# Linear attention into routed experts, one core: transfers, stores and weights sent at other points of the steps, and the placing of a group, one-hots and the late table rearranged

## The chip, the cores and the metric

The kernel runs on one core of a Trainium2 chip. The metric is the time of one execution on the device, in microseconds; lower is better. Engines are named as in the profile: PE (TensorE), PEld (its weight loads), DVE (VectorE), ACT (ScalarE), POOL (GpSimd), SP (SyncE, which here only sends DMAs).

## The reference, cut to what matters

```python
# q, k, v, alpha: (4, 8, 768, 48)
for t in range(S):
    state = alpha[:, :, t, :, None] * state + k_t (outer) v_t
    y[:, :, t] = q_t @ state
x = y as rows: (3072, 384)
skip = x @ w_skip                       # rows with skip <= 0 pass unchanged
e_idx = argmax(x @ w_gate); gate = softmax value at e_idx     # 8 experts
out = x + gate * (relu(x @ w1[e]) @ w2[e])                    # w1: 384x1024, w2: 1024x384
```

All of it is fp32; products run as fp32 (two passes of PE) or as two-term splits (`h` and `l` tiles).

## The kernel before, in words

**Attention.** The 4 x 768 positions are 24 tiles of 128 (`NT`), two batches interleaved, six chunks each; a tile holds all eight heads as four pairs. One loop of `static_path` (L1042) takes a tile i a step and writes the order of every engine by hand. A step holds on PE: `inter` (old state times queries, not in the first chunk), `intra(i, 0)` (first half of scores times values), `scores(i + 1)`, `intra(i, 1)`, `rows(i - 1)` (back to rows, with gate logits), `outer(i)` and `turn_k(i + 1)` (the state's update, not in the last chunk). DVE has `decay` for tile i + 3 in two parts: part 0 scans the decays forward (`pfx`) and POOL scales the queries by it (L281), part 1 scans backward (`sfx`) and POOL scales the keys (L290). Without these keys `scores` of that tile can't start. `causal` (DVE, L321) masks the scores of tile i + 1 into `st`, for which `intra(i + 1, 0)` waits. ACT copies PSUM to SBUF.

**Transfers.** A tile has rows (`qka`: decays, keys, queries; 0.595 MB in two DMAs, `load` parts 0 and 1) and values (`vt`, 0.197 MB, part 3); a finished tile of x is stored (0.197 MB). All go out by SP, in the order of the code. `plan(i)` counts PE's products (an fp32 matmul counts two) and at product 221 + 127n + 4 calls `issue(i, behind)`, whose DMAs wait for that product: rows and values of tile i + 5 (`AHEAD`), then the store of tile i - 2; from step 19 on, where no tiles are left, three pieces of weights (`weight_loads`, 0.262 MB each) instead. `weight_loads` is a generator whose first call sets `self.wait` to None (L656). The prologue sends tiles 0 to 4 without such waits.

**Routing.** The rows fall into groups of tiles, (0, 6), (6, 12), (12, 18), and then late ones, (18, 21), 21, 22, 23. `route` finds the expert (mask `m`) and the gate, six and eight small DVE instructions, handed out by `tick`. `rank` (PE) and `place` (DVE, three instructions) give each row its slot; `one_hot` turns a tile's slots into a 128 x 256 matrix, `marks` spreads ids and gates, and `table` multiplies the two on PE into the table of slots (two small matmuls a tile). A one-hot takes DVE or POOL. `early_rows` gathers expert 0's rows of the first 18 tiles from the table by an indirect DMA of POOL; the late tiles' rows come by `mine` (DVE) and `late_rows` (PE) straight into the first product's input, for which `late_split` makes two-term splits (ACT, POOL). `clear_late` stores zeros over tile 22's rows.

**Experts.** Then each expert is `up`, `down` with weights loaded ahead, split on ACT, DVE and POOL.

Of the kernel before, what the change touches and what calls it, by code (L numbers as in the profile page):

```python
# [10 lines left out]
F32 = mybir.dt.float32  # L11
# [6 lines left out]
ALU = mybir.AluOpType  # L18
# [12 lines left out]
NT = B * C  # L31
NQ = 6
AHEAD = 5
# [33 lines left out]
LATE = 18  # L67
SOLO = 12
EG = 8
WARM = 36  # L70
BLOCK0, BLOCK, PAST, STEP = 221, 127, 4, 112
ORDER = (0, 2, 4, 1, 3, 5)
FIRST = 512
PAUSE = "pause"
# [2 lines left out]
class Kernel:  # L77
# [166 lines left out]
    def load(self, i, part=None, behind=None, eng=None):  # L244
        nc = self.nc
        if i >= NT:
            return
        if part is None:
            for n in range(4):
                self.load(i, n)  # L250
            return
        if part == 0:
            t = self.qkab[i % NQ]
            vt = self.vp.tile([P, DM], F32, name="vt")
            self.work[i] = dict(dec=t[:, 0:DEC], v=vt, qh=t[:, QO:QW].rearrange("p (a t) -> p a t", t=P),
                                kh=t[:, KO:QO].rearrange("p (a t) -> p a t", t=P), begun=set())
        if part == 3:
            ins = (eng or nc.sync).dma_start(out=self.work[i]["v"], in_=self.v[i])
        elif part >= len(WHOLE.get(i, USED)):
            return  # L260
        elif i not in WHOLE:
            rows = USED[part]
            ins = nc.sync.dma_start(out=self.qkab[i % NQ][rows], in_=self.qka[i, rows])
        else:
            s = slice(*WHOLE[i][part])
            ins = (eng or nc.sync).dma_start(out=self.qkab[i % NQ][:, s], in_=self.qka[i, :, s])
        if behind:
            self.follow(ins.ins, behind)
# [265 lines left out]
    def place(self, g):  # L534

        nc = self.nc
        g0, g1 = g
        n = g1 - g0
        pr = self.ranks(g)
        if g0 < LATE:  # L540
            sl = self.sm.tile([P, GT, E], F32, name="sl")[:, :n, :]
        else:
            sl = self.lates[:, g0 - LATE:g1 - LATE, :]
        s2 = self.pslot[:, g0 - SOLO:g1 - SOLO, :] if g0 in (SOLO, NT - 2, NT - 1) else \
            self.late.tile([P, n, 1], F32, name=f"s{g0}")
        for i in range(g0, g1):
            self.work[i]["slot"] = s2[:, i - g0, :]
            self.work[i]["slot0"] = sl[:, i - g0, 0:1]
        yield nc.vector.scalar_tensor_tensor(out=sl, in0=pr, scalar=-BIG, in1=self.m[:, g0:g1, :], op0=ALU.add,
                                             op1=ALU.mult)  # L550
        yield nc.vector.tensor_reduce(out=s2, in_=sl, op=ALU.add, axis=AX.X)
        if g0 < LATE:
            yield nc.vector.memset(pr, 0.0)
# [14 lines left out]
    def marks(self, g):  # L568
        g0, g1 = g
        wide = [P, g1 - g0, E, VW]  # L570
        eng = self.nc.vector if g0 >= SOLO else self.nc.gpsimd
        eng.tensor_tensor(self.mv[:, g0:g1], self.m[:, g0:g1, :].unsqueeze(3).to_broadcast(wide),
                          self.values(g).unsqueeze(2).to_broadcast(wide), ALU.mult)

# [44 lines left out]
    def late_split(self, i, direct=False):  # L619
        nc, w = self.nc, self.work[i]  # L620
        hi, lo = w["parts"] = [self.late.tile([P, DM], F32R, name=f"late{n}{i}") for n in "hl"]
        nc.scalar.copy(out=hi, in_=w["x"])
        if direct:
            pairs = lambda a: a.rearrange("p (a w) -> p a w", a=NP)
            nc.vector.tensor_tensor(pairs(lo), pairs(self.pg[:, 0:NP * RW])[:, :, 0:2 * D], pairs(hi).bitcast(F32),
                                    ALU.subtract)
        else:
            nc.gpsimd.tensor_tensor(lo, w["x"], hi.bitcast(F32), ALU.subtract)

    def late_rows(self, i, ks):  # L630
        w = self.work[i]
# [22 lines left out]
    def weight_loads(self):  # L654

        self.raw, self.wait = {}, None  # L656
        for e in range(E):
            for name, src in (("w1", self.w1), ("w2", self.w2)):
                raw = self.raw[e, name] = self.wraw.tile([P, KT * F], F32, name="raw")
                soon = (e, name) < (1, "w2")  # L660
                step = FIRST if soon else KT * F // 4
                for q in ORDER if name == "w1" and soon else range(KT * F // step):
                    s = slice(q * step, (q + 1) * step)
# [6 lines left out]
    def weight_splits(self):  # L670
# [5 lines left out]
        for e in range(E):  # L676
            for name in ("w1", "w2"):
# [5 lines left out]
                if e == 0 and name == "w1":  # L683
                    yield
                    continue
                for q in ORDER if name == "w1" else range(6):
                    s = slice(q * step, (q + 1) * step)
# [275 lines left out]
    def static_path(self, ctx):  # L963
        tc, nc = self.tc, self.nc
# [3 lines left out]
        self.stay = ctx.enter_context(tc.tile_pool(name="stay", bufs=1))  # L968
        self.banks(ctx)
        loads, splits = self.weight_loads(), self.weight_splits()  # L970
        small = []
        groups = [(0, 6), (6, 12), (12, 18), (18, 21), (21, 22), (22, 23), (23, 24)]

        def advance(it, n=1):
            for _ in range(n):
                next(it, None)

        def tick(n):
            while n and small:
                r = next(small[0], self)  # L980
                if r is self:
                    small.pop(0)
                elif r is PAUSE and n < 50:
                    break
                else:
                    n -= 1

        def bring(i, parts, behind):
            for n in parts:
                self.load(i + AHEAD, n, behind)  # L990

        def issue(i, behind):
            if i + AHEAD < NT:
                bring(i, (0, 1, 3), behind)
            else:
                self.wait = behind
                advance(loads, 3)
            if i < 20:
                self.store(i - 2)

        def plan(i):
            begin = self.products
# [4 lines left out]
        with ExitStack() as st:  # L1007
# [17 lines left out]
                self.load(3, n)  # L1025
            self.load(1, 3)
            self.row_weights()
            self.load(2, 3)
            self.load(4)
            self.load(3, 3)  # L1030
            self.fill(WARM)
            self.scores(0)
            self.cross(0)
# [8 lines left out]
            for i in range(NT):  # L1042
# [2 lines left out]
                    plan(i)  # L1045
                self.inter(i)
                self.intra(i, 0)
                self.fence(i)
                if i:
                    self.keep(i - 1)  # L1050
# [12 lines left out]
                self.scores(i + 1)  # L1063
                self.cross(i + 1)
                if i == 22:
                    self.table((11, 15, 16, 17))
                    self.table_add()
                    self.early_rows(self.numbers(self.tab[:, :, 0:1, :], "ids0", 1))
                self.causal(i + 1)
                if i == 22:  # L1070
                    for _ in self.route(groups[3], True):
                        pass
                tick(2)
                self.decay(i + 3, 0)
                self.intra(i, 1)
                if i == 1:
                    bring(i, (0, 1), self.work[i]["before"])
                self.turn_y(i)
# [3 lines left out]
                    self.logits(i - 1)  # L1082
                if i >= 19:
                    self.store(i - 1)
                if i == 19:
                    self.clear_late(self.work[i - 1]["rowed"])
                self.outer(i)
                if i == 1:
                    bring(i, (3,), self.work[i]["added"])
                if 11 <= i < 22:  # L1090
                    self.table((10, 12, 13, 14) if i == 21 else (i - 11,))
                for g in groups[:3]:
                    if i == g[1] + (2 if g[0] == SOLO else 3):
                        self.rank(g)
                self.carry(i)
                for g in groups[:3]:
                    if i == g[1] + (2 if g[0] == SOLO else 3):
                        for _ in self.place(g):
                            pass
# [4 lines left out]
                tick(1)  # L1104
                if i == 20:
                    tick(99)
                    self.marks(groups[2])
                    for t in range(3):
                        self.one_hot(SOLO + t, nc.vector)
                self.decay(i + 3, 1)  # L1110
                for g in groups[:3]:
                    if i == g[1]:
                        small.append(self.route(g))
                if i in (9, 15):
                    tick(99)
                    self.marks(groups[{9: 0, 15: 1}[i]])
                if 9 <= i < 21:
                    self.one_hot(i - 9, nc.gpsimd)
                if i == 21:
                    for t in range(3):  # L1120
                        self.one_hot(SOLO + 3 + t, nc.vector)
                if i == 11:
                    self.table_add(first=True)
                if i == 22:
                    self.route_one(21)
                tick({18: 6}.get(i, 2))
                if i > LATE:
                    self.late_split(i - 1)
                if i == 19:
                    advance(splits)  # L1130
                if 19 <= i < 23:
                    self.first_split(ORDER[i - 19:i - 18])
                if i == 22:
                    self.first_split((2, 4), nc.gpsimd)
                if i == 21:
                    self.first_split((0,), nc.vector)
                if i == 1:
                    self.rank_constants()
                if i == 2:
# [17 lines left out]
            self.wait = self.ranked  # L1157
            advance(loads, 3)
            self.store(a)
            advance(loads, 2)  # L1160
            self.late_rows(18, range(KT))
            put(g21)
            self.mine(21)
            self.route_one(22)
            self.late_split(22)
            self.first_split((3, 5))
            self.rows(b)
            self.logits(b)
# [9 lines left out]
            self.mine(a)  # L1178
            self.row_copy(b)
            self.store(b)  # L1180
            advance(loads, 2)
            self.late_split(b, True)
            self.early_turn()
            self.late_rank(g23)
# [100 lines left out]
```

## Time and profile before

| | |
|---|---|
| three runs | 267.28, 264.58, 267.57 us, median 267.28 |
| profiled execution | 265.31 us, span 263.6 us |
| busy: PE, PEld, DVE, ACT, POOL | 94%, 88%, 75%, 63%, 67% of the span |
| granted clock of TensorE | 0.993 on average |
| DMA | 59.97 MB, 228 GB/s on average |
| chain that ended last | PE 84%, issue 4%, DVE 4%, POOL 3%, DMA 2% |

The chain follows the work back from the last instruction to what released it; "issue" is time in which the engine waited for nothing that the profile shows. The stages differ: the steps run to about 109 us, the hand-over to 119.7, the experts from there on.

### The profile page before, as it was taken

What the parts mean: (1) busy time and instruction counts of PE and PEld (TensorE: products, weight loads), DVE (VectorE), ACT (ScalarE), POOL (GpSimd) and SP (SyncE); (2) the same over time, 40 slices, a digit from 0 to 9 for tenths busy, and PEclk for the clock granted to TensorE, in tenths of its full rate; (3) what the DMA queues carried; (4) which work ended last, traced back from release to release, by engine and by line L of the source; (5) the groups of instructions that cost most, each with busy time, mean ns of one, the idle gap of its engine ahead of it and who ended that gap; (6) DMA issues with size and microseconds to landing.
All of it is one profiled execution on the core that took longest, in us unless ns stands there. A gap on an engine that the chain in (4) does not pass through costs nothing.

```text
span 263.6 us, 9702 instructions
## 1 busy us (share of the span) xinstructions
PE 247.4 (94%) x3988; PEld 231.6 (88%) x3988; DVE 197.1 (75%) x389; ACT 166.4 (63%) x356; POOL 177.3 (67%) x197
## 2 busy tenths in 40 slices
PE   8679999988999988999999999999999999999990
PEld 6569898976899877789999999999999999999990
DVE  6978889999799889888957728559568496674800
ACT  8657576656567577543646499695995974644600
POOL 6757775779598885999774764848568366546411
PEclk9999999999999999999999999999999999999997
DMA  7987887779788887773499949778698777421000
GB/s 235 325 249 218 278 230 245 216 239 294 223 230 229 266 253 237 218 236 99 133 358 334 323 152 396 267 261 325 196 396 306 228 247 288 152 117 43 3 31 23
DMA packets 25491, 59.97 MB, mean 228 GB/s; under 512 B 4117, under 2 KB 10543, under 8 KB 25440
## 3 DMA queue, kind: packets, MB, share of 16 engines
q1 hardware_dynamic: 23264, 54.23, 63.0%
q0 software_dynamic: 2176, 5.05, 5.6%
q8 instruction: 33, 0.54, 0.9%
q14 instruction: 18, 0.15, 0.2%
HBM read 52.63 MB, written 7.86 MB: 229 GB/s over the span
## 4 chain that ended last, share of the span: by engine, by line
PE 84%; issue 4%; DVE 4%; POOL 3%; DMA 2%; ACT 1%; SPq 0%; POOLq 0%; DVEq 0%
PE ps_h L775 17%; PE ps_v L791 13%; PE ps_c L791 13%; PE ps_y L86 10%; PE ps_s L86 8%; PE ps_g L775 8%; PE ps_g L86 6%; PE ps_v L86 4%; PE ps_k L337 4%; DMA vt<-in_v_dram 2%; PE ps_x L753 2%; ACT st L329 1%; DVE st L321 1%; DVE pfx L277 1%; PE ps_k L86 1%
## 5 line engine op out<-in xcount | busy, mean ns | idle before, releaser
L290 POOL TENSOR_TENSOR qka<-qka,sfx 128x512 f32<-128x512 f32 (+1 forms) x26 | 30.7, 1185 | 12.6 <-DVE sfx L285 9.4
L281 POOL TENSOR_TENSOR qka<-qka,pfx 128x512 f32<-128x512 f32 x24 | 26.2, 1094 | 13.3 <-DVE pfx L277 8.2
L690 POOL TENSOR_TENSOR w2l<-raw,w2h 128x512 fp32r<-128x512 f32 x16 | 21.8, 1361 | 19.2 <-ACT w2h L688 19.1
L797 POOL DMA_INDIRECT out_dram<-o,ids x16 | 17.6, 1102 | 24.6 <-DVE o L795 22.5
L86 PE MATMUL ps_y<-st,vt 64*48 64x64 f32 (+1 forms) x768 | 31.8, 245 | 2.5 <-DMA vt<-in_v_dram 1.3
L690 DVE TENSOR_TENSOR w2l<-raw,w2h 128x512 fp32r<-128x512 f32 x32 | 29.6, 945 | 2.0 <-ACT w2h L688 1.8
L86 PE MATMUL ps_s<-qka 64*64 64x64 f32 (+1 forms) x960 | 26.6, 234 | 4.7 <-issue 3.9
L277 DVE TENSOR_TENSOR_SCAN pfx<-qka,ps_c 128x527 f32<-128x527 f32 x24 | 29.7, 1238 | 1.1 <-DMA qka<-in_qka_dram 1.1
L285 DVE TENSOR_TENSOR_SCAN sfx<-qka,ps_c 128x525 f32<-128x525 f32 x24 | 29.7, 1239 | 0.6
L86 PEld LDWEIGHTS ps_s<-qka 64*64 64x64 f32 x960 | 23.1, 133 | 6.2 <-issue 4.7
L688 ACT CAST w2h<-raw 128x512 fp32r<-128x512 f32 x48 | 27.2, 617 | 0.0
L86 PEld LDWEIGHTS ps_y<-st,vt 64*48 64x48 f32 x768 | 22.3, 120 | 4.5 <-DVE st L321 3.0
L600 POOL DMA_INDIRECT xr<-out_dram,ids x18 | 21.9, 1217 | 5.0 <-issue 4.2
L690 DVE TENSOR_TENSOR w1l<-raw,w1h 128x512 fp32r<-128x512 f32 x27 | 23.5, 888 | 2.2 <-ACT w1h L688 1.7
L329 ACT COPY st<-ps_s 64x256 f32<-64x256 f32 x48 | 17.7, 368 | 11.6 <-PE ps_s L86 11.0
L688 ACT CAST w1h<-raw 128x512 fp32r<-128x512 f32 x42 | 23.6, 622 | 0.0
L779 ACT ACTIVATE hh<-ps_h 128x480 fp32r<-128x480 f32 x22 | 12.6, 571 | 17.1 <-PE ps_h L775 14.6
L86 PE MATMUL ps_g<-xw,xt 112*64 112x105 f32 x384 | 23.0, 259 | 0.3 <-issue 0.2
L775 PE MATMUL ps_h<-xh,w1h 128*128 128x240 f32 x132 | 22.6, 276 | 0.2 <-ACT xh L650 0.2
L690 POOL TENSOR_TENSOR w1l<-raw,w1h 128x512 fp32r<-128x512 f32 x15 | 19.7, 1312 | 4.4 <-ACT w1h L688 4.2
L321 DVE COPY_PREDICATED st<-mask,ps_s 128x512 f32<-128x512 uint8 x24 | 17.7, 738 | 6.5 <-ACT st L329 6.3
L775 PE MATMUL ps_h<-xh,w1l 128*128 128x240 f32 x132 | 22.6, 276 | 0.0
(176 smaller groups left out, 690.4 us busy)
## 6 DMA issues: line engine op xcount, KB each, us to landing
raw<-in_w_dram SPq DMA_DIRECT2D x52, 384.0 KB, 5.5
qka<-in_qka_dram SPq DMA_DIRECT2D x22, 387.8 KB, 4.2
vt<-in_v_dram SPq DMA_DIRECT2D x24, 192.0 KB, 4.8
out_dram<-x SPq DMA_DIRECT2D x24, 192.0 KB, 4.6
raw<-in_w_dram SPq DMA_DIRECT2D x18, 256.0 KB, 4.6
alpha<-in_nat_dram SPq DMA_DIRECT2D x8, 576.0 KB, 4.4
qka<-in_qka_dram SPq DMA_DIRECT2D x22, 193.9 KB, 5.1
qka<-in_qka_dram SPq DMA_DIRECT2D x2, 263.5 KB, 2.7
```

Of the source, the lines that this page charges most:

```text
L86: ins = self.nc.tensor.matmul(out, **operands)
L277: nc.vector.tensor_tensor_scan(pfx[:, 0:DEC], dec, self.floor.to_broadcast([P, DEC]), FLOOR, ALU.mult, ALU.max)
L281: nc.gpsimd.tensor_tensor(w["qh"], w["qh"], pfx.rearrange("p (a w) -> p a w", w=SEG)[:, :, 1:P + 1], ALU.mult)
L285: nc.vector.tensor_tensor_scan(sfx[:, 2:DEC][:, ::-1], dec[:, 2:DEC][:, ::-1], self.floor.to_broadcast([P, DEC - 2]), FLOOR, ALU.mult, ALU ...
L290: eng.tensor_tensor(w["kh"][:, a], w["kh"][:, a], sfx[:, a], ALU.mult)
L321: self.nc.vector.copy_predicated(st[:, :, :, 0:HP], self.mask, ps[:, :, :, 0:HP])
L329: self.nc.scalar.copy(out=st[:HP, :, n * NX:(n + 1) * NX, HP:], in_=ps[t, :, :NX, HP:])
L600: return [self.nc.gpsimd.indirect_dma_start(out=xr[:n, j, :], out_offset=None, in_=self.out[0:end, :], in_offset=bass.IndirectOffsetOnAxis ...
L688: nc.scalar.copy(out=hi[:, s], in_=raw[:, s])
L690: eng.tensor_tensor(lo[:, s], raw[:, s], hi[:, s].bitcast(F32), ALU.subtract)
L775: nc.tensor.matmul(ps[:, u, :], lhsT=a[:, k, f * P:(f + 1) * P], rhs=b[:, k, :], start=(n == 0), stop=(n == len(order) - 1), skip_group_ch ...
L791: nc.tensor.matmul(ps[:r], lhsT=a[:, f, js], rhs=b[:, f, :], start=(n == 0), stop=(n == 3 * FT - 1), skip_group_check=True)
```

## The change

- **Prologue.** Values 2 and 3, rows and values 4 leave the prologue; they go out in step 0 after `intra(0, 0)`, rows first, then values 2, 3, 4.
- **`issue`.** Values go first, and from step 11 on they come three tiles ahead instead of five, so steps 10 and 11 send none; stores are one more tile behind in steps 11 to 19, so step 11 sends none. Weights: 2, 1, 1 and 3 pieces in steps 19 to 22 instead of 3 each; the tail sends 3, 5 and 4 instead of 3, 2 and 2.
- **First group.** `place`, `marks` and the first one-hot move from the end of step 9 to the middle of step 10.
- **Third group.** Its slots lie in SBUF (before in PSUM). Step 20: `marks` goes to POOL, the three one-hots on DVE go, hot 11 comes ahead of `decay`. Step 21: hots 12 and 13 on POOL, 14 to 17 on DVE; only tile 10 in the table. Step 22: the table of tiles 11 to 17, behind the late group's `route` and `intra(22, 1)`.
- **Small moves.** `late_split` leaves its POOL part to `late_low`, a step later for tiles 19 and 20; DVE's `first_split` of piece 0 goes from step 21 to step 22; `clear_late` from step 19 to step 21.

```diff
+LAG = 10
...
-        if part == 0:
+        if i not in self.work:
             t = self.qkab[i % NQ]
...
-        s2 = self.pslot[:, g0 - SOLO:g1 - SOLO, :] if g0 in (SOLO, NT - 2, NT - 1) else \
+        s2 = self.pslot[:, g0 - SOLO:g1 - SOLO, :] if g0 >= NT - 2 else \
             self.late.tile([P, n, 1], F32, name=f"s{g0}")
...
-        eng = self.nc.vector if g0 >= SOLO else self.nc.gpsimd
+        eng = self.nc.vector if g0 >= LATE else self.nc.gpsimd
...
-        else:
-            nc.gpsimd.tensor_tensor(lo, w["x"], hi.bitcast(F32), ALU.subtract)
+
+    def late_low(self, i):
+        hi, lo = self.work[i]["parts"]
+        self.nc.gpsimd.tensor_tensor(lo, self.work[i]["x"], hi.bitcast(F32), ALU.subtract)
...
+        small, lag = [], dict(v=2 + AHEAD, x=0)
...
         def issue(i, behind):
-            if i + AHEAD < NT:
-                bring(i, (0, 1, 3), behind)
-            else:
+            weights = i + AHEAD >= NT
+            if weights:
                 self.wait = behind
-                advance(loads, 3)
-            if i < 20:
-                self.store(i - 2)
+                advance(loads, (2, 1, 1, 3)[i + AHEAD - NT])
+            while lag["v"] < min(NT, i + AHEAD + 1 - (0 if i < LAG else 3 if weights else 2)):
+                self.load(lag["v"], 3, behind)
+                lag["v"] += 1
+            if not weights:
+                bring(i, (0, 1), behind)
+            while lag["x"] < min(LATE, i - 1 - (LAG < i < NT - AHEAD + 1)):
+                self.store(lag["x"])
+                lag["x"] += 1
...
             self.row_weights()
-            self.load(2, 3)
-            self.load(4)
-            self.load(3, 3)
             self.fill(WARM)
...
                 self.intra(i, 0)
+                if i == 0:
+                    self.load(4, 0, self.work[0]["before"])
+                    self.load(4, 1)
+                    for t in (2, 3, 4):
+                        self.load(t, 3)
...
                 if i == 22:
-                    self.table((11, 15, 16, 17))
+                    for _ in self.route(groups[3], True):
+                        pass
+                    self.intra(i, 1)
+                    self.table(range(11, LATE))
                     self.table_add()
                     self.early_rows(self.numbers(self.tab[:, :, 0:1, :], "ids0", 1))
                 self.causal(i + 1)
-                if i == 22:
-                    for _ in self.route(groups[3], True):
+                if i == 10:
+                    for _ in self.place(groups[0]):
                         pass
+                    tick(99)
+                    self.marks(groups[0])
+                    self.one_hot(0, nc.gpsimd)
                 tick(2)
                 self.decay(i + 3, 0)
-                self.intra(i, 1)
+                if i < 22:
+                    self.intra(i, 1)
...
                 if 11 <= i < 22:
-                    self.table((10, 12, 13, 14) if i == 21 else (i - 11,))
+                    self.table((i - 11,))
...
                 if i == 20:
                     tick(99)
+                    self.one_hot(11, nc.gpsimd)
                     self.marks(groups[2])
-                    for t in range(3):
-                        self.one_hot(SOLO + t, nc.vector)
                 self.decay(i + 3, 1)
...
-                if 9 <= i < 21:
+                if 10 <= i < 20:
                     self.one_hot(i - 9, nc.gpsimd)
                 if i == 21:
-                    for t in range(3):
-                        self.one_hot(SOLO + 3 + t, nc.vector)
+                    for t in range(SOLO, LATE):
+                        self.one_hot(t, nc.gpsimd if t < SOLO + 2 else nc.vector)
...
                 if i == 22:
                     self.route_one(21)
+                    self.first_split((0,), nc.vector)
                 tick({18: 6}.get(i, 2))
                 if i > LATE:
                     self.late_split(i - 1)
+                for t in {19: (18,), 21: (19,), 22: (20, 21)}.get(i, ()):
+                    self.late_low(t)
```

## Rows read from the trace of the kernel before

**Rows 1.** Windows by stage: engines' busy us, instructions, clock, DMA share, GB/s.

```profile
10.70:109.00 98.30, 92.39 (x2750) 80.75 (x2750) 88.93 (x194) 63.20 (x164) 73.20 (x95) 1.00 0.81 242
...
109.00:119.70 10.70, 10.17 (x140) 8.86 (x138) 8.93 (x43) 5.49 (x13) 10.18 (x11) 1.00 0.81 261
119.70:263.60 143.90, 137.36 (x1016) 136.28 (x1016) 90.90 (x142) 90.10 (x170) 86.20 (x76) 0.99 0.60 211
```

**Rows 2.** Waits: who waited for whom, us in total, times, longest us.

```profile
PEld ps_s L86 <- issue: 4.7, 4, 1.7
```

**Rows 3.** Timeline of PE: start us, us, instructions; idle before, releaser in brackets.

```profile
16.57 0.34 PE L86 MATMUL ps_s<-qka 64*64 64x64 f32 x7 [1.53 <-issue]
...
60.01 0.92 PE L86 MATMUL ps_y<-st,vt 64*48 64x128 f32 x16 [0.16 <-issue]
...
66.37 0.86 PE L86 MATMUL ps_s<-qka 64*64 64x128 f32 x36 [1.41 <-issue]
...
96.83 0.70 PE L86 MATMUL ps_s<-qka 64*64 64x64 f32 x29 [0.97 <-issue]
...
105.61 0.65 PE L86 MATMUL ps_y<-st,vt 64*48 64x128 f32 x16 [0.89 <-DVE st L321]
...
107.25 0.37 PE L86 MATMUL ps_v<-mv,hot 128*128 128x40 bf16 x8
...
112.38 0.38 PE L86 MATMUL ps_s<-mine,lateh 128*128 128x240 f32 x1 [0.17 <-DVE mine L557]
```

**Rows 4.** The page's DMA queues: packets, MB, share of 16 engines.

```profile
q8 instruction: 33, 0.54, 0.9%
```

**Rows 5.** DMA queues from 13.4 to 15.3 us.

```profile
q8 instruction: 1, 0.02, 5.9%
```

**Rows 6.** DMA queues: all from 60.3 to 63.9 us; then 63.9 to 64.8.

```profile
q1 hardware_dynamic: 378, 0.95, 92.6%
...
q8 instruction: 1, 0.02, 6.1%
```

**Rows 7.** DMA queues from 71.9 to 73.0 us.

```profile
q8 instruction: 1, 0.02, 5.7%
```

**Rows 8.** DMA queues: all from 91.5 to 94.5 us.

```profile
q1 hardware_dynamic: 433, 0.69, 78.1%
```

**Rows 9.** Timeline of SP: start us, us, DMAs sent.

```profile
10.15 1.15 SPq L263 DMA_DIRECT2D qka<-in_qka_dram  x2
...
58.85 1.12 SPq L263 DMA_DIRECT2D qka<-in_qka_dram  x2
...
61.18 1.14 SPq L263 DMA_DIRECT2D qka<-in_qka_dram  x2
...
90.89 1.45 SPq L664 DMA_DIRECT2D raw<-in_w_dram  x3
```

**Rows 10.** Timeline of DVE, steps 20 to 22.

```profile
102.38 0.41 DVE L572 TENSOR_TENSOR mv<-m,vals 128x240 bf16<-128x240 bf16 x1
...
103.70 1.24 DVE L285 TENSOR_TENSOR_SCAN sfx<-qka,ps_c 128x525 f32<-128x525 f32 x1
...
106.80 0.68 DVE L700 TENSOR_TENSOR w1l<-raw,w1h 128x512 fp32r<-128x512 f32 x1
...
108.91 0.17 DVE L460 TENSOR_REDUCE lmx<-ps_c 128x3 f32<-128x24 f32 x1
...
110.00 0.18 DVE L465 SCALAR_TENSOR_TENSOR m<-ps_c,eq 128x24 bf16<-128x24 f32 x1
```

**Rows 11.** Timeline of POOL, step 20.

```profile
105.02 1.27 POOL L290 TENSOR_TENSOR qka<-qka,sfx 128x512 f32<-128x512 f32 x1 [3.13 <-DVE sfx L285]
```

**Rows 12.** One-hots and marks on POOL: ns min/median/max, first, last start.

```profile
L566 POOL TENSOR_SCALAR hot<-slots,s x16: 912/922/950, 57.4 to 119.3; 128x256 bf16<-128x256 f32 x16
...
L572 POOL TENSOR_TENSOR mv<-m,vals x2: 588/592/596, 56.9 to 82.5; 128x240 bf16<-128x240 bf16 x2
```

**Rows 13.** Line of the weight splits, DVE: ns min/median/max.

```profile
L690 DVE TENSOR_TENSOR w2l<-raw,w2h x32: 675/727/1534, 123.8 to 248.4; 128x512 fp32r<-128x512 f32 x32
```

More of the change, by code (lines that the diff above doesn't have):

```diff
@@ L970, in static_path @@
         loads, splits = self.weight_loads(), self.weight_splits()
-        small = []
+        small, lag = [], dict(v=2 + AHEAD, x=0)
         groups = [(0, 6), (6, 12), (12, 18), (18, 21), (21, 22), (22, 23), (23, 24)]
@@ L1084, in static_path @@
                     self.store(i - 1)
-                if i == 19:
+                if i == 21:
                     self.clear_late(self.work[i - 1]["rowed"])
@@ L1095, in static_path @@
                 self.carry(i)
-                for g in groups[:3]:
+                for g in groups[1:3]:
                     if i == g[1] + (2 if g[0] == SOLO else 3):
@@ L1113, in static_path @@
                         small.append(self.route(g))
-                if i in (9, 15):
+                if i == 15:
                     tick(99)
-                    self.marks(groups[{9: 0, 15: 1}[i]])
-                if 9 <= i < 21:
+                    self.marks(groups[1])
+                if 10 <= i < 20:
                     self.one_hot(i - 9, nc.gpsimd)
                 if i == 21:
-                    for t in range(3):
-                        self.one_hot(SOLO + 3 + t, nc.vector)
+                    for t in range(SOLO, LATE):
+                        self.one_hot(t, nc.gpsimd if t < SOLO + 2 else nc.vector)
                 if i == 11:
@@ L1134, in static_path @@
                     self.first_split((2, 4), nc.gpsimd)
-                if i == 21:
-                    self.first_split((0,), nc.vector)
                 if i == 1:
@@ L1159, in static_path @@
             self.store(a)
-            advance(loads, 2)
+            advance(loads, 5)
             self.late_rows(18, range(KT))
@@ L1165, in static_path @@
             self.late_split(22)
+            self.late_low(22)
             self.first_split((3, 5))
@@ L1180, in static_path @@
             self.store(b)
-            advance(loads, 2)
+            advance(loads, 4)
             self.late_split(b, True)
```

## The prediction

> **What bounds the kernel now.** I first cut the span at the stages [rows 1]. The expert stage, 119.7 to 263.6 us, has TensorE busy for 137.4 of 143.9 us and the change touches nothing in it, so it keeps its length. The 24 attention steps run to about 109 us, the hand-over to the experts to 119.7 us. In the stretch 10.7 to 109 TensorE is busy 92.4 of 98.3 us: what can be won there is the 5.9 us of gaps. The list of waits names the largest cause, "issue", a wait for nothing that the profile shows [rows 2]. In TensorE's order of time they are three gaps, 1.53 us before 16.57, 1.41 before 66.37 and 0.97 before 96.83 [rows 3]: 3.91 us together.
>
> Next I asked what those three places share. Counted in products (an fp32 matmul is two), they fall at 221, 1618 and 2507, that is at 221 + 127n, the number on which the kernel's own `plan` is built. The instruction queue moved 33 packets, 0.54 MB, so 16 KB each [rows 4]: one for each such block. 2750 products take 92.4 us [rows 1], so a block lasts 4.3 us. Looking at the queues in short windows dates the packets. The block missing at 16.57 came in a packet between 13.4 and 15.3 [rows 5], the one missing at 66.37 between 63.9 and 64.8 [rows 6]; TensorE went on 1.3 to 1.6 us after the packet. A packet takes about 1 us, so a fetch that is asked for when one block begins must start some 1.8 us later at most (4.3 - 1.0 - 1.5). In an untroubled step it does: block boundary 4.2 us after 66.37, packet from 71.9 on [rows 7], 1.4 us later. For step 12 the boundary is the fourth product of the step that begins at 60.01 [rows 3], and the packet started 3.9 us later; in between 0.95 MB of data passed [rows 6], 0.26 MB a us. So the fetch stands behind the data that SP had sent before it.
>
> The last gap that matters is at 105.61, 0.89 us for tile 22's masked scores [rows 3], and the hand-over behind it.
>
> **The change, part by part.** Times are of the profiled execution, 265.31 us (263.6 of span, 1.7 around it). The four times known are 264.58, 265.31, 267.28 and 267.57; their middle is 266.3, so I sum on 265.3 and add 1.0 at the end.
>
> *Start-up.* Before, SP sent tile 4's rows from 10.15 on [rows 9], ahead of or beside the fetch asked for at about 10.8 (15.04, the start of the gap, less 4.3); values 2, 4 and 3 stood around them. Now these wait for the end of the first half of step 0, product 100, six products past the boundary. The fetch meets little data and the 1.53 us go. But then seven transfers follow at once: rows 4, values 2, 3, 4 and rows 5, which now stand behind the values: 2 x 0.595 + 3 x 0.197 = 1.78 MB by the shapes. At about 0.57 us a transfer [rows 9] SP needs from 11.4 to 15.4 for them. At the next boundary, 15.0, at most 3.6 us x 0.26 = 0.95 MB are moved, so about 0.8 MB stand before that fetch: 3.1 us if it waits for all, 1.4 if it does as in the untroubled step [rows 7]. Against the 1.8 allowed, TensorE then waits 0 to 1.3 us at product 348; 1.6 at most if the queue also starts a us late. I take 0.6, between the ends, nearest to the untroubled step. Gain 0.9 us, bounds -0.1 and 1.5. No tile comes late by it: rows 4 are first scanned in step 1, values 2 used in step 2.
>
> *Steps 10 to 12.* Before, two steps' transfers went out back to back, from 58.85 and 61.18 [rows 9]. The change leaves out the values in steps 10 and 11 (later values come three tiles ahead, not five) and one store: 3 x 0.197 = 0.59 MB less, 2.3 us at 0.26 MB a us. The fetch was 3.9 - 1.8 = 2.1 us too late, so the gap of 1.41 goes. Bounds 0.8 and 1.5; I take 1.4. Values then have more than two steps to land; if that cover went, first-half products would wait for them.
>
> *Steps 18 to 20.* Three weight pieces go out from 90.89 [rows 9], the boundary is near 91.5 (95.86 - 4.3), and 0.69 MB pass before the packet [rows 8]. The first call of `weight_loads` clears `self.wait`, so these pieces aren't held. Two of three are sent before the boundary; the change keeps just these two, at the same place, and leaves out the third, which stood behind the fetch anyway. A store is in front as before. I take 0 for the gap of 0.97, bounds 1.0 gained and 0.6 lost (a second store close by).
>
> *Placing the first group half a step later.* The same vector and GpSimd instructions in another order; tile 11's masked scores come a little earlier, and tile 12's, which set the start of step 12, stand behind the same sum of vector work. 0, bounds 0.3 either way.
>
> *Steps 20 to 22 and the hand-over.* In step 20 the vector engine did group 3's marks and three one-hots from 102.38 to 103.70 ahead of the scan for tile 23 [rows 10]; GpSimd waited 3.13 us for that scan, and only then, at 105.02, made the keys of tile 23 [rows 11]. Marks and hots 12 and 13 go to GpSimd at 0.59 and 0.92 each [rows 12], with hot 11 ahead of the keys. The scan starts 1.3 us earlier, the marks fit into the wait, so the keys too come 1.3 earlier, at 103.7 to 105.0, and the gap before 105.61 goes. Then GpSimd makes hots 12 and 13, to 106.8. The table of tiles 11 to 17 (14 matmuls instead of 8) now follows the second half of step 22 and waits for hot 13: 106.8 to 107.3, against 107.25 to 107.6 before [rows 3]. Here 0.9 of the 1.3 is lost. Next on the vector engine came tile 23's mask, then the third late group's routing, 108.91 to 110.18, six instructions [rows 10], which held tile 21's routing, `place`, `mine` and TensorE at 112.38 [rows 3]. The routing now runs during the wait for hot 13 (1.27 off that path); `first_split`, 0.68 [rows 10], enters it. 0.4 + 1.27 - 0.68 = 1.0, plus 0.1 for a shorter queue of products: 1.1 us. Bounds: 0.9 lost, 1.5 gained.
>
> *Without a price.* Late weights (7 instead of 12 pieces by step 22) have until the expert stage's second products; the zeroing store two steps later lands before the early gather; `late_low` follows its own step's work on GpSimd, which loses 1.8 us in hots and marks and wins 1.3 us of waiting. Each is hidden by the hand-over; if the gather came late, its turning would wait, up to 1 us, inside the bounds above.
>
> Sum: 0.9 + 1.4 + 0 + 0 + 1.1 = 3.4; 265.3 - 3.4 + 1.0 = 262.9 us.
>
> **The rivals.** (1) *All fetch waits go*, that at 96.83 and the one I put at product 348 too: 3.9, and 1.5 at the end, 5.4 us: 260.9. For it: the margins are tenths of a us. Against: two weight pieces still stand before the fetch.
>
> (2) *Data is not what the fetch waits for.* Then the three gaps stay, and only the hand-over gains: 265.3 - 1.1 + 1.0 = 265.2. Against it speak the 0.95 MB that passed first [rows 6]. For it: the fetches have their own queue [rows 4]. The Trainium skill ("DMA: Bandwidth & Descriptors", "Queues, rings and completion order") says that a DMA engine takes turns between its queues packet by packet, by which a fetch would wait for a packet or so whatever SP had sent; the 3.9 us of step 12 do not agree.
>
> (3) *The vector engine and GpSimd block each other.* Group 3's slots move from PSUM to SBUF, so hots 14 to 17 on the vector engine now read two SBUF tiles while GpSimd makes hots 12, 13 and a split. In the expert stage a vector instruction with two SBUF inputs has a median of 0.73 us and a longest of 1.53 [rows 13]. If each hot waits for one GpSimd instruction, 0.3 + 0.92 + 0.92 + 1.0 = 3.1 us are added, of which 1.1 are hidden: the hand-over loses 0.9 instead of winning 1.1. 265.3 - 0.9 - 1.4 + 0.9 + 1.0 = 264.9. Against it: the `first_split` at 106.80 took its 0.68 while a GpSimd one-hot ran. The Trainium skill ("SBUF — State Buffer", "Who interferes with whom") has a vector instruction with two SBUF inputs and a GpSimd one that reads SBUF wait for each other in full; the 1.53 agrees, the 0.68 does not.
>
> (4) *Slower: the late burst is never caught up.* From 11.4 on transfers run 0.8 MB behind; if the queue stays that long, the fetches of the next three blocks and of two in steps 18 to 20 start past the 1.8 us, which is where it decides. A late block costs 3.91 / 3 = 1.3 us; five cost 6.5. 265.3 - 3.9 + 6.5 - 1.1 + 1.0 = 267.8. Against: a step brings 0.99 MB, and 4.3 us move 1.1.
>
> **How the numbers follow.** Forecast 0.47, (1) 0.17, (2) 0.14, (3) 0.14, (4) 0.08. The likeliest gives 262.9, by its bounds 261.3 to 264.5. The range 260.2 to 266.2 takes in (2) and (3) and most of (1); left out are (4) and the far tails, under 0.2. 2% of the median 267.28 is 5.3 us, about what a measurement can tell from no change here (the three runs lie 3 us apart): under 261.9 lie most of (1) and a fifth of the forecast, 0.24; over 272.6 only the tail of (4), 0.02; the rest 0.74.
>
> **What would show it.** No issue gap at product 221 and at most a short one at 348; none in step 12, with its instruction packet within 1.8 us of the boundary; one of about a us still in step 20; the keys of tile 23 made near 103.7 less what was won before; one-hots on the vector engine at 0.41; the first `mine` product 7.6 us after those keys begin (7.4 before). Wrong if the gaps stand elsewhere, if hots stretch, or if the expert stage changes.

## The result and the profile after

The changed kernel takes 263.78 us (median of 20 runs, 261.71 to 265.47) against 266.19 for the kernel before on the same chip (20 runs, 264.58 to 270.93): ratio 0.992, 95% interval 0.9896 to 0.9943, so 2.1 us less by the ratio and 2.4 by the medians; the ratio leaves out executions more than 1.5% above the fastest of their kernel, the medians take all. Timed a second time it was 0.9906 [0.9865, 0.9947]. Forecast were 262.9 us and a gain of 3.4: the sign was right and so were most of the places, the sum was half as large again as what came.

Its profiled execution took 264.53 us (span 262.7). By stage (the columns of [rows 1]; the attention steps and the hand-over end a microsecond earlier than before, the experts last as long):

```profile
10.70:108.00 97.30, 93.42 (x2766) 81.77 (x2768) 88.73 (x196) 63.98 (x165) 75.66 (x98) 1.00 0.77 233
108.00:118.70 10.70, 9.39 (x130) 8.27 (x122) 8.53 (x37) 5.29 (x13) 10.37 (x11) 1.00 0.75 231
118.70:262.70 144.00, 137.35 (x1016) 136.27 (x1016) 90.81 (x142) 90.11 (x170) 86.92 (x76) 0.99 0.63 221
```

TensorE in order of time, to be held against [rows 3]:

```profile
18.82 0.92 PE L87 MATMUL ps_s<-qka 64*64 64x64 f32 x29
20.54 0.28 PE L87 MATMUL ps_s<-qka 64*64 64x64 f32 x3 [0.80 <-issue]
...
65.44 0.86 PE L87 MATMUL ps_s<-qka 64*64 64x128 f32 x38
...
95.99 0.70 PE L87 MATMUL ps_s<-qka 64*64 64x64 f32 x29 [0.64 <-issue]
...
110.80 0.65 PE L87 MATMUL ps_y<-st,vt 64*48 64x64 f32 x16 [1.06 <-ACT spot L406]
...
111.45 0.36 PE L87 MATMUL ps_s<-mine,lateh 128*128 128x240 f32 x1
```

The gap at product 221 is gone, one of 0.80 stands at product 348 instead; step 12 has none; step 20 keeps 0.64 of its 0.97; the wait for tile 22's masked scores, 0.89 before, is gone, but a new stop of 1.06 us stands at 110.80. The stop is that execution's own: the second profile of the same kernel (below) has none there. What it was is open.

The instruction packets (queues in short windows, as [rows 5] to [rows 8]; first the data between a block boundary and the packet, then the window with the packet): step 12, boundary at 61.05, and step 20, boundary at 90.93.

```profile
q1 hardware_dynamic: 119, 0.40, 64.0%
...
q8 instruction: 1, 0.02, 5.5%
...
q1 hardware_dynamic: 250, 0.46, 71.6%
...
q8 instruction: 1, 0.02, 5.8%
```

In step 12, 0.40 MB passed before the packet (0.95 in [rows 6]); it started 1.8 us after the boundary, just what the prediction allowed, instead of 3.6 (the prediction's 3.9 counts from 60.01, where the step begins; its fourth product, the boundary, starts at 60.29). In step 20 it was 0.46 MB instead of 0.69 [rows 8], and 2.4 us instead of 3.1.

### The profile page after: what moved, and what is told of

Same layout as the page of the kernel before. It is cut to its first block, busy times and chain, and to the rows that moved or that the text cites. A ratio compares the mean times of both kernels' runs of the same rounds, so it can differ in the third digit from the quotient of the medians.

```text
span 262.7 us, 9712 instructions
## 1 busy us (share of the span) xinstructions
PE 249.1 (95%) x3988; PEld 232.8 (89%) x3988; DVE 195.9 (75%) x386; ACT 166.2 (63%) x356; POOL 180.5 (69%) x200
## 4 chain that ended last, share of the span: by engine, by line
PE 89%; POOL 3%; DVE 2%; issue 1%; ACT 1%; DMA 1%; SPq 0%; POOLq 0%; DVEq 0%
PE ps_h L778 17%; PE ps_v L794 13%; PE ps_c L794 13%; PE ps_y L87 11%; PE ps_g L87 10%; PE ps_s L87 8%; PE ps_g L778 8%; PE ps_v L87 4%; PE ps_k L338 4%; PE ps_x L756 2%; POOL hot L567 1%; DVE st L322 1%; ACT st L330 1%; DMA out_dram<-x 1%; PE ps_k L87 1%
## 5 line engine op out<-in xcount | busy, mean ns | idle before, releaser
L87 PE MATMUL ps_y<-st,vt 64*48 64x64 f32 (+1 forms) x768 | 32.5, 245 | 3.0 <-issue 1.2
```

Source lines behind the costliest of these rows:

```text
L87: ins = self.nc.tensor.matmul(out, **operands)
```

## The experiments

To compare executions I use one table, worked out from the starts of TensorE's products: us from product 94 to 475 (start-up), to 1491, to 1618 (step 12), to 2380, to 2507 (step 20), and on to the first `mine` product.

```
                           94-475 475-1491 1491-1618 1618-2380 2380-2507 2507-mine
before                     13.93   35.42     6.10      25.05     5.40     15.54
before, second profile     13.30   35.02     5.28      25.01     4.39     16.02
e1 prologue alone          12.87   35.44     4.70      24.83     6.17     15.57
e2 transfers alone         13.47   35.11     4.29      25.09     5.33     15.55
e3 the rest alone          15.72   34.99     4.73      25.00     4.64     15.12
e4 all but the prologue    13.62   34.94     4.37      24.81     5.08     14.75
after                      14.01   35.99     4.50      25.38     5.07     15.45
after, second profile      13.92   35.13     4.36      25.66     4.79     14.71
e5 burst                   12.91   35.60     4.72      27.43     4.80     15.03
e6 five x buffers          13.55   35.10     4.48      25.67     6.14     14.67
e7 PSUM slots              12.73   35.85     4.34      25.11     5.60     14.57
e8 weights held            14.08   34.78     4.54      25.55     4.15     15.69
e9 values spread           13.68   35.03     4.26      25.79     4.51     14.71
e10 all together           13.92   34.91     4.55      25.15     4.15     15.69
```

From the first `mine` product to the experts it is 7.3 to 7.5 us in all, and the expert stage 143.8 to 144.6.

**The change in parts (e1 to e4, run together).** The prologue's part on the kernel before:

```diff
-            self.load(2, 3)
-            self.load(4)
-            self.load(3, 3)
...
+                if i == 0:
+                    self.load(4, 0, self.work[0]["before"])
...
```

> The kernel before with the prologue's part of the change alone (rows and values 4, values 2 and 3 go out in step 0 after the first half of its products). By the sum of the prediction: the gap of 1.53 us before product 221 goes, one of about 0.6 comes at product 348, 0.9 us faster in all (bounds -0.1 and 1.5). By the trace of the changed kernel, in which product 348 passes at 20.54 us against 20.75 before and product 475 at 25.06 against 24.86: the gap only moves, 0 to 0.2 us. By the theory that fetches don't wait for data: 1.53 us stay at product 221, 0 us.

0.9963 [0.9929, 0.9998], 1.0 us. No gap at 221 or 348 in this execution. With the same prologue, or its values spread (e9, e10 below), six of eight other profiles show a pause of 0.3 to 1.4 us (between the starts of products) at 348 or 475, so one profile could not size it.

The new `issue` and the tail's weights on the kernel before:

```diff
+            while lag["v"] < min(NT, i + AHEAD + 1 - (0 if i < LAG else 3 if weights else 2)):
...
+            while lag["x"] < min(LATE, i - 1 - (LAG < i < NT - AHEAD + 1)):
...
```

> The kernel before with the new order of values, stores and weights in the steps and the tail alone (prologue, placing, one-hots and table as before). By the sum of the prediction: the gap of 1.41 us in step 12 goes, that of 0.97 in step 20 stays, 1.4 us faster (bounds 0.8 and 1.5 and, with step 20, up to 2.4). By the trace of the changed kernel: 1.6 from step 12 and 0.3 from step 20, up to 1.9, less what its short waits near 37.9 and 42.7 us take (0.45 and 0.6) if they belong to this part. By the theory that fetches don't wait for data: 0 us, and the gap before the scores of step 12 still 1.4.

0.9907 [0.9874, 0.994], 2.5 us (interval 1.6 to 3.3): the largest part, as much as the whole change, and more than the 1.4 to 1.9 expected. Step 12 falls to 4.29 us; step 20 keeps its gap.

The rest on the kernel before (the whole change with prologue, `issue` and weights undone), and the whole change with the prologue alone undone:

```diff
-                    self.load(4, 0, self.work[0]["before"])
-                    self.load(4, 1)
-                    for t in (2, 3, 4):
-                        self.load(t, 3)
```

> The kernel before with the rest of the change alone (first group placed in step 10, third group's slots, marks and one-hots, the late table, late_low, clear_late, first_split); all loads, stores and weights go out as before. By the sum of the prediction: 1.1 us faster (bounds -0.9 and 1.5), all of it between the keys of tile 23 and the first product of the experts. By the rival in which the vector engine and GpSimd block each other: 0.9 us slower, one-hots 14 to 17 at 1 us and more. By the trace of the changed kernel: 1.5 won at the keys, 0.5 to 1.3 given back up to the first product of mine, 0.2 to 1.0 in all.

> The changed kernel with the prologue as before. By the sum of the prediction it is 0.9 us slower than the changed kernel, 2.5 us faster than before. By the trace of the changed kernel, where the gap only moves from product 221 to 348: as fast as the changed kernel, 2.4 us faster than before, or up to 0.5 faster still if the burst of step 0 also made the short waits near 37.9 and 42.7 us. It also tells whether the stop of TensorE from 109.5 to 110.8 us in the changed kernel's profile recurs: if it belongs to the new order, it is there again (about 1.1 us before the second half of tile 23's products); if it was that one execution's, it is not.

e3: 0.9948 [0.9908, 0.9988], 1.4 us. e4: 0.9906 [0.987, 0.9942], as the whole change, so inside it the prologue's part is worth nothing that can be measured, and the stop at 110.80 does not recur. By themselves the parts give 0.4 + 0.9 + 0.5 = 1.8%, together 0.8 to 0.9%; the intervals don't exclude a plain sum of e2 and e3 for e4 (1.5% against 0.6 to 1.3), but the whole falls short of the three.

e1 and e3 leave the transfers of step 12 as they were, yet that step took 4.70 and 4.73 us, not 6.10. The gap of [rows 3] is not a constant.

**A burst put where there was none (e5).**

```diff
+        self.extra = BLOCK0 + 12 * BLOCK - 100
...
+            for q in range(6):
+                s = slice(q * FIRST, (q + 1) * FIRST)
+                more = self.nc.sync.dma_start(out=self.spare[:, s], in_=self.w1[E - 1, :, s])
```

> The changed kernel with six more loads of 0.262 MB (weights that nothing reads) sent by SP 100 products before the block boundary at product 1745, in a stretch without gaps. If a fetch stands behind the data sent before it: 1.57 MB in 3.4 us, of which 0.26 MB a us are moved, so 0.7 MB and more are left at the boundary; the packet that started 1.57 us after it starts 3 to 4.5 us after it, and TensorE waits 1.2 to 2.7 us at product 1872. If queues take turns packet by packet: the packet starts 1.4 to 2.2 us after the boundary as its neighbours do, and no gap.

1.0023 [0.999, 1.0057]: the whole gain is lost. SP's burst, then the queues from the boundary of product 1872 (73.15 us) to the packet and in the packet's window, then TensorE:

```profile
67.19 2.83 SPq L97 DMA_DIRECT2D raw<-in_w_dram  x6
```

```profile
q1 hardware_dynamic: 617, 1.36, 102.5%
...
q8 instruction: 1, 0.02, 5.3%
```

```profile
73.14 0.74 PE L87 MATMUL ps_s<-qka 64*64 64x64 f32 x31 [0.34 <-issue]
...
79.14 0.74 PE L87 MATMUL ps_s<-qka 64*64 64x128 f32 x31 [1.48 <-issue]
```

At 1745 the packet started 2.5 us after the boundary, and TensorE waited 0.34 us for it, both less than expected (3 to 4.5, 1.2 to 2.7); at 1872 it started after 3.6 us and 1.36 MB, and that gap is the large one. This stretch takes 27.43 us instead of 25.4. The sizes follow from what SP had sent and the queue had not yet moved when the boundary passed: 0.84 MB at 1745, where more than half of the burst was still to be sent, and 1.20 at 1872, with the next tile behind the burst; 0.75 and 1.36 MB moved before the packets. Counted in this way over all 14 profiles (boundaries 221 to 2507), the two amounts agree to 0.15 MB at 231 of 266 boundaries. So here a fetch waits for the data that SP had sent before it, and a burst can hand its lateness to the next block. That settles rival 2.

**The hand-over (e6, e7) and step 20 (e8).** Five buffers for x; the slots of tiles 14 to 17 copied to PSUM; the late weights held:

```diff
-        self.xp = st.enter_context(tc.tile_pool(name="xp", bufs=4))
+        self.xp = st.enter_context(tc.tile_pool(name="xp", bufs=5))
```

> The changed kernel with five buffers for x instead of four, so that the copy of tile 21 to x doesn't wait for the late split of tile 19 on GpSimd. If that wait (1.37 us on ScalarE in two profiles) holds the hand-over: logits, routing of tile 21, first_split and mine come up to 1.3 us earlier, TensorE's 0.26 us before the first product of mine goes and 0.3 to 0.4 us are won between product 2507 and it (15.45 and 14.76 us in the two profiles). If TensorE's own products set that time: less than 0.1 us.

```diff
+                        if g[0] == SOLO:
+                            nc.vector.tensor_copy(self.pslot[:, 2:6, :], self.work[SOLO]["slots"][:, 2:6, :])
```

> The changed kernel with the slots of tiles 14 to 17 copied to PSUM after place (one small vector instruction), so that one-hots 14 to 17 read one SBUF tile each. If vector instructions with two SBUF inputs and GpSimd hold each other up: those four fall from 1.97 us in all to about 1.3, GpSimd's hots 12 and 13 from 2.29 to 1.84, and TensorE's wait of 0.76 us for hot 13 shrinks by 0.4. If not: 1.97, 2.29 and 0.76 stay.

```diff
-        self.raw, self.wait = {}, None
+        self.raw = {}
```

> The changed kernel with the first two late weight pieces held behind the product that the plan names (the first call of weight_loads no longer clears the wait). If the fetch of step 20 stands behind these two pieces (0.52 MB, 2 us): the packet that started 2.4 to 2.7 us after the boundary at product 2380 starts within 1.8 us, the gap of 0.9 us before the scores of step 20 goes, 0.9 us faster than the changed kernel. If it stands behind something else: the gap stays, 0 us.

e6: 0.9937 [0.9905, 0.9968]. The wait for the late split is gone, but ScalarE then waits as long for TensorE, and so 14.67 us instead of 14.71 to 14.75: the split moved behind the one-hots is covered (0.05 us).

```profile
107.19 0.48 ACT L427 COPY x<-ps_g 128x384 f32<-128x384 f32 x1 [1.32 <-PE ps_g L87]
```

e7: 0.9915 [0.9882, 0.9948], no more than the changed kernel. One-hots by line (ns min/median/max), first the changed kernel's second profile, then e7, where GpSimd's two took 1.83 us and TensorE's wait for them fell from 0.76 to 0.29:

```profile
L565 DVE TENSOR_TENSOR hot<-slots,s x4: 410/511/758, 102.1 to 103.6; 128x256 bf16<-128x256 f32 x4
...
L567 POOL TENSOR_SCALAR hot<-slots,s x18: 910/922/1350, 56.6 to 116.9; 128x256 bf16<-128x256 f32 x18
```

```profile
L566 DVE TENSOR_TENSOR hot<-slots,ps_c x6: 408/410/412, 102.1 to 115.4; 128x256 bf16<-128x256 f32 x6
...
L568 POOL TENSOR_SCALAR hot<-slots,s x18: 912/924/940, 56.1 to 116.5; 128x256 bf16<-128x256 f32 x18
```

```profile
101.28 1.29 POOL L291 TENSOR_TENSOR qka<-qka,sfx 128x512 f32<-128x512 f32 x1 [0.41 <-DVE sfx L286]
102.54 1.83 POOL L568 TENSOR_SCALAR hot<-slots,s 128x256 bf16<-128x256 f32 x2
...
104.42 0.47 PE L87 MATMUL ps_v<-mv,hot 128*128 128x40 bf16 x12 [0.29 <-POOL hot L568]
...
108.86 0.38 PE L87 MATMUL ps_s<-mine,lateh 128*128 128x240 f32 x1 [0.26 <-DVE mine L559]
```

With one SBUF input each the vector one-hots are back at 0.41 us and no GpSimd one-hot is above 0.94; with two, two of the four stretched, to 0.76 and 0.61, and one of GpSimd's to 1.35. So rival 3's mechanism is real, at 0.47 us of TensorE's wait instead of 2 to 3; only 0.14 of it shows in the hand-over (14.57 against 14.71), as the keys of tile 23 came 0.33 us later after product 2507, behind the wait of 0.41 for the scan. The Trainium skill ("SBUF — State Buffer", "Who interferes with whom") has such a pair lock each other out; these rows agree that they do, and show that the price here was a partial wait on each side, not a full one for each instruction.

e8: 0.9929 [0.9893, 0.9964], nothing gained. The packet came 1.0 us after the boundary of step 20 and its gap went (4.15 us), but the hand-over grew to 15.69:

```profile
102.66 0.93 PE L87 MATMUL ps_s<-qka 64*64 64x128 f32 x40 [0.33 <-POOL qka L291]
```

```profile
101.32 1.28 POOL L291 TENSOR_TENSOR qka<-qka,sfx 128x512 f32<-128x512 f32 x1
```

GpSimd has no wait left before the keys of tile 23 and TensorE waits for them; near the end of step 20 TensorE's weight loads had already waited 0.25 us for ScalarE's `spot`. Without the gap the keys came no earlier: they begin 11.79 us after product 2380, against 11.72 and 11.44 in the changed kernel's two profiles. GpSimd's own work sets them, and TensorE's gap had covered it: the 0.6 to 0.9 us won in step 20 (4.79 and 5.07 in the changed kernel's profiles) came back as 0.98 behind it. (The kernel before does the same in its second profile: 4.39, then 16.02.)

**Both kernels again, the burst spread, and all together.** The first two are unchanged kernels.

> The changed kernel as it is, once more, beside the other three. If the stop of TensorE at 109.5 us and the short gaps near 37.9 and 42.7 us belong to the change, they are there again; if they are draws of one execution, the stop is gone and the short gaps stand at other blocks. Between product 2507 and the first product of mine 14.7 us instead of 15.45. Its ratio to the kernel before again near 0.992.

> The kernel before once more, for a second profile. If its gap in step 12 is there in every execution: 6.1 us from product 1491 to 1618 as in its first profile. If it is drawn anew: 4.3 to 6.1, 4.7 as in the two experiments that left the transfers of step 12 alone. From product 2507 to the first product of mine 15.55.

Step 12 of the kernel before took 5.28 us, its gap 0.50 in place of the 1.41 of [rows 3]:

```profile
64.18 0.86 PE L86 MATMUL ps_s<-qka 64*64 64x128 f32 x36 [0.50 <-issue]
```

The changed kernel, 0.9906 [0.9865, 0.9947], drew gaps at 348, 475, 2380 and 2507, none near 37.9, 42.7 or 109.5; its hand-over (14.71):

```profile
101.25 1.29 POOL L291 TENSOR_TENSOR qka<-qka,sfx 128x512 f32<-128x512 f32 x1
102.51 2.30 POOL L567 TENSOR_SCALAR hot<-slots,s 128x256 bf16<-128x256 f32 x2
```

```profile
104.87 0.47 PE L87 MATMUL ps_v<-mv,hot 128*128 128x40 bf16 x12 [0.76 <-POOL hot L567]
...
109.31 0.38 PE L87 MATMUL ps_s<-mine,lateh 128*128 128x240 f32 x1 [0.26 <-DVE mine L558]
```

```diff
-                    for t in (2, 3, 4):
-                        self.load(t, 3)
+                    self.load(2, 3)
...
-                    bring(i, (3,), self.work[i]["added"])
+                    for t in (4, 5, 6):
+                        self.load(t, 3, self.work[i]["added"] if t == 4 else None)
...
+                    self.load(3, 3)
```

> The changed kernel with values 3 sent behind rows 5 and values 4 behind the update of step 1, so that 0.39 MB fewer stand before the fetch of the block at product 348. If that burst makes the gap: none at product 348, 94 to 475 in 12.7 to 12.9 us as in the executions that drew none (14.0 and 14.1 in those that drew one), some 0.5 us faster than the changed kernel on average. If the start-up's gaps come from something else: 12.7 to 14.1 as before.

0.9926 [0.9888, 0.9964], start-up 13.68: the expectation failed. SP shows what came instead: the next rows simply move up, and the values follow as a burst of their own.

```profile
16.05 1.12 SPq L264 DMA_DIRECT2D qka<-in_qka_dram  x2
17.27 3.11 SPq L259 DMA_DIRECT2D vt<-in_v_dram  x4
```

e10 is e7, e8 and e9 in one, with five x buffers and this:

```diff
-                for t in {19: (18,), 21: (19,), 22: (20, 21)}.get(i, ()):
+                for t in {21: (18, 19), 22: (20, 21)}.get(i, ()):
```

> The changed kernel with the spread values, the held weight pieces, five buffers for x, the PSUM slots of tiles 14 to 17, and the late split of tile 18 moved behind GpSimd's one-hots 12 and 13. By the sum: 1.0 from the gap of step 20, of which the hand-over gave 0.9 back because GpSimd was busy without a break up to the keys of tile 23; moving the late split away there gives 0.3 of it, the PSUM slots 0.47: 18.9 to 19.2 us from product 2380 to the first product of mine (19.8 in four executions of the new order), with 0.5 from the start 1.1 to 1.4 us faster than the changed kernel. If GpSimd still sets that stretch: 19.8, and 0.5 us.

0.9956 [0.9929, 0.9982], no faster than the changed kernel. Two waits stand where the gain was expected: ScalarE waited 0.45 us for the held weights, and TensorE 0.67 for ScalarE's `spot` behind that; and the late splits on GpSimd, now beside the vector engine's `ids` (0.16 us in the other profiles of the new order), held it for 1.03:

```profile
103.72 1.96 POOL L632 TENSOR_TENSOR latel<-x,lateh 128x384 fp32r<-128x384 f32 x2
```

```profile
104.66 1.03 DVE L597 SCALAR_TENSOR_TENSOR ids<-tab 128x2 int32<-128x2 f32 x1
```

```profile
94.45 0.65 PE L87 MATMUL ps_y<-st,vt 64*48 64x64 f32 x16 [0.67 <-ACT spot L406]
...
106.38 0.65 PE L87 MATMUL ps_y<-st,vt 64*48 64x128 f32 x16 [0.65 <-DVE st L322]
```

No version tried is clear of the changed kernel.

## Why the prediction was right, and where its sizes were off

**The mechanism** held in the steps. Over all 14 profiles, at 18 boundaries each (221 to 2507 without 1364, behind which every kernel pauses, however early the packet), I dated the packet asked for there and looked for a pause at the next boundary. TensorE paused over 0.3 us behind none of the 200 packets that had landed within 3.0 us, behind 8 of 21 that landed at 3.0 to 3.3, and 28 of 31 later. Product 221 itself, whose packet is asked for at 94, fits too: it pauses in the five profiles with the old prologue (3.6 to 4.5 us) and in none of the nine others (1.9 to 2.4). The prediction's limit, 1.8 us and a packet of 1.0, was 2.8. e5 made such a gap, e8 removed one. One stop does not fit: that of 1.06 us in the changed kernel's first profile stands at such a boundary too, product 2888, but its packet had landed 2.2 us after the boundary at which it was asked for, as early as in blocks without a pause.

Two of the prediction's own signs of being wrong came up as well, at a small price: gaps stood at other boundaries, and one-hots stretched (0.76 and 0.61 us instead of 0.41).

**Start-up, 0.9.** The seven profiles with the new prologue average 13.44 us, the five with the old one 14.01: 0.6, inside the bounds, of which 0.4 hangs on e3's slow start (below); e4 finds nothing in the runs. The gap put at product 348, 0.6, measured 0.80 and 0.25 in the two profiles of the changed kernel.

**Steps 10 to 12, 1.4.** Mis-sized: 0.76 measured. The four profiles with the old transfers average 5.20 us for that block, the ten with the new ones 4.44. The gap went as forecast, but what it was worth was read from one execution that had drawn the largest of four.

**Steps 18 to 20, 0.** Right: 5.15 us on average with the old pieces, 5.17 with the new (held ones left out).

**First group placed later, 0.** Within 0.3: TensorE's pause ahead of the first half of step 12's products rose from 0.16 to 0.44, the stretch around it did not.

**Hand-over, 1.1.** The keys of tile 23 begin 8.18 us after product 2507 before, 6.65 after: 1.53 earlier (1.3 forecast). From keys to `mine` 8.06 us, 7.6 forecast: the difference is e7's 0.47, and e7 itself gives 7.58. Net 0.83 (15.54 to 14.71). The forecast's sentence on GpSimd, "loses 1.8 us in hots and marks", leaves out the marks, 0.59 [rows 12]; by rows it is 2.4. Taken with step 20, with which it trades, 20.99 us on average in four profiles of the old order and 19.92 in seven of the new (e7, e8 and e10 left out): 1.07.

**What had no term.** From 1618 to 2380 the new order takes 25.36 us (nine profiles without e5's), the old one 24.97: 0.39 lost, in blocks of steps 13 to 19 whose packets came slightly late. The table says more: the loss is there only where the new prologue and the new transfers stand together. Those seven profiles (e5's aside) take 25.11 to 25.79 us; the new transfers with the old prologue (e2, e4) 25.09 and 24.81, and the four with the old transfers 24.83 to 25.05. So some 0.5 us of what the prologue wins at the start is lost again later, which agrees with e4, in which the prologue is worth nothing. How the start reaches steps 13 to 19 is open.

Sum: 0.6 + 0.8 + 0 + 1.1 - 0.4 = 2.1, the time measured; that it comes out to the tenth is luck. The terms are means of a few executions that differ by up to 1.8 us in one stretch, and for e2 they give 0.4 to 0.8 us where its times gave 2.5 [1.6, 3.3]; the clock in the last section can be a small part of that difference, the rest is open. The forecast came out inside its range, but one step of it did not hold, "they are three gaps", summed to "3.91 us together": it took one execution's gaps for the kernel's. Rival 4's late blocks did occur (four in each profile of the changed kernel), but at 0.2 to 0.8 us instead of 1.3, so they only shortened the gain. Rival 1 fell with step 20 and product 348. For rival 2 the Trainium skill ("DMA: Bandwidth & Descriptors", "Queues, rings and completion order") has queues take turns by the packet; e5's 1.36 MB ahead of one packet do not agree.

## What to carry to other kernels

The waits for instructions differed from one execution to the next of the same kernel (1.41 and 0.50 us in step 12): before such gaps are summed, profile the kernel more than once, or look how near its other blocks come to the limit. A burst of DMAs moved off one block lands on another, as at product 348 here and in e9, unless the queue has a stretch with nothing to send. Where one engine's stall is removed, look which engine comes no earlier for it: here GpSimd's keys took back all that step 20 had won.

## What the runs showed of the hardware that I had not expected

In e3's profile the gap at product 221 (1.42 us before 16.62) was followed by 3.4 us, from 16.88 on, at half the granted clock, with no gap in the records. Windows of the start, the columns of [rows 1]:

```profile
16.00:18.00 2.00, 1.38 (x29) 1.03 (x31) 0.59 (x2) 0.73 (x2) 1.43 (x2) 0.72 0.78 252
18.00:20.00 2.00, 2.00 (x30) 2.00 (x30) 1.97 (x3) 0.97 (x2) 0.05 (x1) 0.50 0.44 96
20.00:22.00 2.00, 2.00 (x57) 1.75 (x58) 1.74 (x4) 0.69 (x2) 1.04 (x1) 0.93 0.77 248
```

30 products in 2 us at 0.50 (1.2 of 2.4 GHz); block 221 to 348 took 5.74 us, 4.2 in the kernel before. The kernel before had a gap as long there [rows 3] and kept its clock, so the drop cost 1.5 us in this execution; that the gap brought it on is not shown.

The times of the other executions, which come with a mean granted clock each, say that such executions are not rare, and which part of the change bears on them. e3's profiled execution has a mean of 0.986, the other 13 profiled ones, none of which drops between 10 and 255 us, 0.991 to 0.997. Among the timed executions that a ratio uses and that list it, 21 of 98 with the old transfers (the kernel before, e1, e3) have 0.990 or less, but 1 of 111 with the new ones; on three chips the kernel before took 0.9, 1.4 and 1.9 us longer in them (medians 265.66 against 264.75, 265.25 against 263.90, 265.69 against 263.83). With the new transfers and the old prologue, gap at 221 included, it is none of 12 (e2, e4); with the new prologue and the old transfers 1 of 10 (e1). So it is the new order of transfers that the higher clock goes with, though for e1, e2 and e4 the counts are small; and some 0.2 to 0.4 us of the gain (17 of the 80 executions of the kernel before at 0.9 to 1.9 us, an estimate) are not in gaps at all. Where the clock fell in the executions without a profile is not known.
